# A two-block kernel with a written-out instruction order: the first third of the order is replaced

## The chip, the cores and the metric

The kernel runs on one core of a Trainium2 chip. The metric is the device time of one execution in microseconds (us). Five engines work side by side, each through its own instructions in a fixed order: TensorE (PE, with its weight loads shown as PEld), VectorE (DVE), ScalarE (ACT), GpSimd (POOL) and SyncE (SP), which here only issues DMAs. POOL issues DMAs too, and ACT issues eight at the start. An instruction waits, and everything behind it on its engine with it, until the results that it reads are there and the memory that it writes is free.

## The reference

Two blocks follow each other. The first is a linear recurrence over 768 time steps for 4 x 8 pairs of batch and head, with a 40 x 40 state in each:

```python
for t in range(S):
    kt, vt, rt = (k[:, :, t], v[:, :, t], r[:, :, t])
    wt, at, bt = (w[:, :, t], a[:, :, t], b[:, :, t])
    y[:, :, t] = np.einsum('bhd,bhde->bhe', rt, state)
    Sa = np.einsum('bhde,bhe->bhd', state, at)
    state_decay = state * wt[:, :, None, :] - np.einsum('bhd,bhe->bhde', Sa, bt)
    state = state_decay + np.einsum('bhd,bhe->bhde', vt, kt)
...
xn = x / rms * rms_g
g = xn @ w_gate
silu = g * (1.0 / (1.0 + np.exp(-g)))
val = xn @ w_val
return (silu * val @ w_out).astype(np.float32)
```

The second block (the lower five lines) takes the 3072 tokens of 320 values that the recurrence yields, normalises them, and puts them through a gated feed-forward layer with 1536 inner columns. The four weight arrays of this layer arrive as 64-bit floats.

## The kernel before

The 768 steps are cut into 24 chunks of 32. Inside a chunk the recurrence becomes matrix products and a triangular inverse. A chunk `c` goes through three stages, and every pair of chunks feeds the second block. In the text a piece is named by its stage and chunk, as "inverse 3".

- **front c** loads w, a, k, b, v of the chunk, turns them on PE, multiplies the decays up level by level (DVE, ACT), and forms products of keys and removals (`gramk`, 32 matmuls each on PE). At the end it writes a triangular matrix to DRAM (`sB<-LT`) and reads it back in another layout (`M<-sB`).
- **inverse c** inverts that triangle with short DVE operations. For the first four chunks (`early_inverse`) only two half-size triangles are inverted on DVE, which go out and back through DRAM (`sY<-M`, then four reads `M<-sY`); two matmul pieces `inv` on PE, with an ACT copy between them, join the halves. The first of the two reads what the four reads bring.
- **main c** applies the inverse to the incoming state, which waits for main c-1, updates the state, and computes the outputs of the chunk (`score`, `level`, `y0`), which are normalised and turned into `xg`.
- **feed g** runs for each pair of chunks through 12 blocks of inner columns: load a weight block (`wf<-sW`), products `h64` and `h`, Silu on ACT (`sg`), product with the value half on DVE (`hT`), product `out` on PE that accumulates in `po`.
- **narrow n** (24 pieces of work, all in the early part) turns the 64-bit weights into 32-bit ones: it loads raw words into a `wf` tile, takes three ACT and three DVE operations, and writes the result to the DRAM tile `sW`, from which `feed` reads.

None of this is issued in the order in which it is written. Each helper (`tt`, `copy`, `pe`, `dma` and so on) only records a piece in a `Plan`, with what it must wait for. At the end `plan.issue(ORDER, PAIRS)` goes through a long string of numbers. Each number is an offset from the first piece not yet issued, and says which piece is issued next, on whatever engine it belongs to. A dash issues a fill, a matmul that no result needs, which keeps PE at work:

```python
for word in order.split():
    if word == "-":
        self.order.append(None)
        self.warm()
        continue
    i = first + int(word)
...
plan.warm = lambda: nc.tensor.matmul(po_[:, 0, DM:DM + P], ident, ident, start=False, stop=False, skip_group_check=True)
```

The second string, `PAIRS`, says in which of three PSUM tile pairs each of 499 blocks of PE results (a "room") is placed. Between its issue and its use a piece has no other tie than its data, its memory and its neighbours on the engine. So `ORDER` sets for every engine and every DMA queue what stands behind what. All DVE operations carry line L444 in the profile, ACT copies L467, activations L464, scalings L470, DMA issues L483, matmuls L486, turns L489 and fills L1015, since the helpers stand there.

Of the kernel before, what the change touches and what calls it, by code (L numbers as in the profile page):

```python
# [33 lines left out]
78 84 86 83 5 88 73 58 85 74 60 77 59 87 89 53 61 76 90 4 75 80 43 6 7 62 8 334 - - - - - - 93 9 10 79 11 201 12 557  # L34
13 214 14 567 18 15 16 44 558 17 95 19 209 566 20 - 97 94 21 23 568 22 200 24 96 25 108 578 100 98 199 335 26 101 569
202 113 107 106 - - - - 102 54 577 112 213 111 125 210 122 110 124 586 103 120 46 559 2 57 104 52 560 109 598 105 - -
- - - - - - - - 114 588 561 45 118 119 27 562 123 116 392 589 563 132 204 121 117 134 212 129 131 136 135 47 564 570
597 203 - - - - - - - - - - 336 115 587 571 394 133 137 144 126 145 155 130 337 211 565 146 573 383 574 572 - 219 55
141 3 579 384 575 143 609 51 128 582 607 222 1005 127 580 281 608 583 48 220 381 339 234 81 142 390 239 221 251 - - -
- - - - - - - - - - 153 263 282 581 380 272 226 91 338 227 393 138 584 154 379 238 576 590 206 237 223 140 247 249 56  # L40
593 82 591 139 49 585 594 224 - 325 216 150 31 382 233 232 29 592 38 236 149 235 326 147 156 595 215 250 248 148 28
260 259 391 271 205 606 30 42 - - - - - - - - - 228 389 599 617 41 229 245 40 246 244 92 600 243 32 602 629 39 601 230
65 1006 1136 34 231 1414 627 37 66 152 603 35 50 - - - - - - - 240 151 610 71 604 628 611 64 613 63 241 252 262 36 614
258 69 242 356 261 0 69 255 256 71 254 617 611 398 269 32 625 98 67 253 66 267 266 206 268 604 252 207 278 400 614 636
217 399 647 401 263 216 405 279 156 595 413 877 406 648 402 265 157 868 417 0 0 257 719 0 258 269 0 242 454 706 265 0
0 0 263 0 - - - - - 242 247 0 262 0 263 462 0 243 462 0 0 272 0 460 0 0 266 0 264 0 275 239 0 461 248 0 245 441 238 0
86 247 441 0 229 95 93 441 0 229 93 95 0 242 0 467 450 0 268 227 - - - - - - - - - - - - - - - 236 467 0 437 467 0 0
38 0 254 435 0 209 233 88 252 199 249 232 - - 243 89 248 246 208 247 198 445 0 434 257 244 467 469 258 243 - 254 259
470 463 468 464 435 93 465 0 268 93 259 255 3 444 2 254 1 94 214 263 269 0 91 682 261 92 93 258 94 692 466 95 260 96
691 97 467 469 473 - - - - - 0 97 680 469 460 467 440 98 99 0 472 99 469 - 0 99 501 0 0 0 400 0 0 0 0 0 0 0 - - - - 20  # L50
0 0 0 0 19 150 147 0 17 150 0 144 0 375 356 0 13 352 358 16 359 356 - - - - - 25 357 17 26 360 80 148 394 149 18 29
150 81 396 151 192 393 70 27 395 31 152 71 30 153 361 154 386 0 35 31 - 189 27 388 154 386 389 190 36 387 37 45 192
390 34 391 155 32 33 156 396 157 158 0 396 398 3 158 - - - - - 37 399 2 397 1 159 45 160 40 0 157 34 37 551 158 159
560 160 396 210 549 38 429 39 161 552 212 42 430 162 561 397 163 43 164 550 213 44 559 165 45 - - - - - 0 561 45 46 0
164 565 165 166 167 168 46 169 566 740 567 580 739 47 572 568 729 573 429 - - - - - 0 729 582 429 47 583 48 431 0 381
- - 136 383 0 520 576 136 518 577 139 383 686 138 545 534 384 119 696 546 544 558 0 686 541 119 542 566 518 553 696
527 526 - - - - - - - 522 136 529 554 141 523 565 539 530 142 538 120 524 540 - - - - 145 525 537 534 154 152 148 536
149 556 555 121 - - 157 146 535 122 147 564 165 125 550 551 150 552 123 155 153 692 124 151 164 682 160 549 0 688 160
0 160 689 161 0 163 0 554 506 41 553 42 564 43 420 507 996 44 555 995 45 509 421 13 508 435 436 571 422 14 384 437 374
495 46 573 839 447 572 383 574 578 448 840 432 586 579 47 373 591 590 575 829 434 589 599 600 830 433 602 577 612 444  # L60
0 575 442 600 846 602 440 47 0 582 583 - 15 836 440 585 835 491 16 609 586 846 613 621 578 622 47 48 593 49 596 444
594 - 50 595 579 443 53 492 51 580 52 0 493 580 135 0 312 313 314 0 314 315 316 317 318 319 320 321 3 322 39 323 324
38 325 326 36 327 328 329 452 0 329 3 0 3 355 467 451 468 465 0 325 352 462 355 467 326 354 327 448 328 458 31 329 353
330 331 468 332 476 364 460 333 473 475 334 0 440 425 301 331 302 436 7 0 452 436 0 1 446 2 332 436 444 445 0 440 338
449 298 340 334 0 316 329 330 342 32 381 331 341 0 333 379 30 332 331 440 369 329 441 314 368 - - - - 0 442 294 441
518 295 0 297 295 335 0 0 331 27 37 46 1 28 336 337 29 36 30 338 31 34 341 2 342 294 3 0 647 439 440 441 637 442 443
444 646 335 31 445 446 645 336 447 448 449 634 28 0 607 310 35 311 606 0 258 307 7 610 308 29 618 259 416 309 27 417
28 418 310 419 619 821 281 420 421 620 633 812 621 625 311 811 638 - 475 0 311 625 821 281 636 635 312 0 648 644 1 647
0 418 0 - - - - - 4 642 643 654 619 309 5 310 653 825 418 665 657 419 824 420 26 666 421 422 815 9 27 29 44 814 30 45
28 42 423 0 616 423 5 32 424 9 6 33 470 425 617 10 0 419 303 420 421 465 0 614 300 301 418 615 419 0 401 12 0 282 598  # L70
32 597 590 21 401 402 33 403 464 3 22 591 0 219 0 399 587 0 599 0 7 586 217 8 0 598 8 9 0 457 598 396 599 32 9 35 397
398 0 0 - - - - - - - - - 582 23 388 22 389 390 32 597 600 3 604 598 33 599 447 14 603 583 391 4 15 612 17 0 579 13 11
387 388 14 20 389 15 390 417 0 38 22 20 37 23 2 418 35 390 417 391 47 419 392 393 420 394 21 395 396 588 0 27 23 2 396
0 21 585 600 601 599 586 27 25 0 31 418 27 25 393 394 595 419 395 28 52 396 29 596 422 397 597 607 398 604 0 397 571 0
394 571 391 577 0 363 1 5 387 2 577 394 364 392 0 362 377 386 0 384 394 507 569 377 392 506 568 387 571 497 401 647
570 496 402 0 394 416 395 377 705 396 713 359 400 397 378 712 0 400 713 401 701 402 654 714 403 404 0 702 655 1142 570
1143 656 571 701 572 654 573 574 8 575 404 576 577 0 577 639 404 578 579 405 580 2 406 581 582 407 583 584 357 585 408
781 586 360 587 717 588 358 3 0 588 358 589 639 718 975 590 3 717 591 0 980 588 637 719 715 981 589 720 0 587 967 406
715 713 728 986 416 724 588 976 401 589 714 729 0 984 589 740 590 591 974 402 721 403 662 401 592 722 752 717 726 738
# [968 lines left out]
```

## Time and profile before

| | |
|---|---|
| median of three runs | 1079.54 us (1079.13 to 1092.11) |
| the profiled execution | 1085.4 us, of which the span of the core's instructions is 1083.6 us |
| PE busy | 1021.8 us, 94% of the span |
| DVE busy | 851.0 us, 79% |
| ACT, POOL busy | 469.3 us and 308.9 us |
| granted PE clock, mean | 0.98 of full speed |
| DMA | 143.35 MB, mean 132 GB/s |

The profiled execution took 5.9 us more than the median. The busy share is an average over two quite different parts. In the first 240 us PE is idle or runs fills for a good part of the time, and the granted clock falls to half in five stretches. After that PE is hardly ever idle.

### The profile page before, as it was taken

What the parts mean: (1) busy time and instruction counts of PE and PEld (TensorE: products, weight loads), DVE (VectorE), ACT (ScalarE), POOL (GpSimd) and SP (SyncE); (2) the same over time, 40 slices, a digit from 0 to 9 for tenths busy, and PEclk for the clock granted to TensorE, in tenths of its full rate; (3) what the DMA queues carried; (4) which work ended last, traced back from release to release, by engine and by line L of the source; (5) the groups of instructions that cost most, each with busy time, mean ns of one, the idle gap of its engine ahead of it and who ended that gap; (6) DMA issues with size and microseconds to landing.
All of it is one profiled execution on the core that took longest, in us unless ns stands there. A gap on an engine that the chain in (4) does not pass through costs nothing.

```text
span 1083.6 us, 53520 instructions
## 1 busy us (share of the span) xinstructions
PE 1021.8 (94%) x23408; PEld 842.4 (78%) x23408; DVE 851.0 (79%) x2861; ACT 469.3 (43%) x1043; POOL 308.9 (29%) x554
## 2 busy tenths in 40 slices
PE   8877997899999999999999999999999999999998
PEld 7776776777877778787778778877878878887876
DVE  7877868885878988788798789979889889787321
ACT  5856755543543434433434334434335334432211
POOL 9714422120432141341332232332322331210000
PEclk9869998999999999999999999999989999999999
DMA  9965457775464483655555555555545555444242
GB/s 183 203 136 142 70 124 187 203 156 158 122 143 119 103 170 89 151 117 132 125 141 122 130 134 124 116 136 138 137 102 132 121 136 143 113 114 115 79 149 77
DMA packets 172458, 143.35 MB, mean 132 GB/s; under 512 B 125504, under 2 KB 143872, under 8 KB 172224
## 3 DMA queue, kind: packets, MB, share of 16 engines
q1 hardware_dynamic: 153856, 116.96, 42.2%
q0 software_dynamic: 16192, 22.64, 11.7%
q8 instruction: 184, 3.01, 1.2%
q10 hardware_dynamic: 2176, 0.33, 0.2%
q14 instruction: 50, 0.41, 0.1%
HBM read 123.86 MB, written 15.99 MB: 129 GB/s over the span
## 4 chain that ended last, share of the span: by engine, by line
PE 72%; DVE 12%; ACT 5%; DMA 4%; issue 4%; SPq 2%; POOL 0%; DVEq 0%; ACTq 0%; POOLq 0%
PE ps L486 49%; PE po L486 12%; PE ps L489 10%; DVE LT L444 2%; SPq L483 2%; DVE As L444 1%; DVE tmp L444 1%; DVE y L444 1%; DVE K L444 1%; DVE Yi L444 1%; ACT K L467 1%; DMA wf<-in_moe_w_val_dram 1%; PE po L1015 1%; DMA M<-sY 1%; ACT ex L464 1%
## 5 line engine op out<-in xcount | busy, mean ns | idle before, releaser
L486 PE MATMUL ps<-xg,wf 128*128 128x256 f32 (+1 forms) x1728 | 353.9, 391 | 5.2 <-DVE xg L444 2.1
L486 PEld LDWEIGHTS ps<-xg,wf 128*128 128x128 f32 (+1 forms) x1728 | 261.1, 188 | 60.3 <-issue 18.5
L486 PE MATMUL po<-wf,hT 128*128 128x320 f32 x576 | 180.0, 445 | 1.1 <-issue 0.6
L464 ACT ACTIVATE sg<-ps 128x256 f32<-128x256 f32 x144 | 53.7, 382 | 228.0 <-PE ps L486 215.5
L444 DVE TENSOR_TENSOR tmp<-Yi,M 128x60 f32<-128x60 f32 (+24 forms) x620 | 130.0, 210 | 20.1 <-DMA M<-sB 5.9
L483 POOL DMA_DIRECT2D VU<-in_v_dram x92 | 53.2, 584 | 310.3 <-PE ps L486 170.2
L444 DVE TENSOR_TENSOR Yi<-Yi,tmp 128x60 f32<-128x60 f32 (+24 forms) x620 | 129.8, 210 | 13.8
L486 PEld LDWEIGHTS po<-wf,hT 128*128 128x128 f32 x576 | 102.0, 189 | 36.6 <-issue 2.8
L444 DVE TENSOR_TENSOR hT<-ps,sg 128x256 f32<-128x256 f32 x144 | 59.6, 419 | 66.9 <-ACT sg L464 65.8
L444 DVE TENSOR_TENSOR K<-K,T 128x512 f32<-128x512 f32 (+1 forms) x192 | 93.1, 495 | 14.7 <-PE ps L486 5.7
L486 PEld LDWEIGHTS ps<-Ab,K 40*64 40x64 f32 x4608 | 78.6, 140 | 29.3 <-issue 10.2
L486 PE MATMUL ps<-Ab,K 40*64 40x56 f32 x4608 | 88.5, 227 | 8.9 <-issue 2.6
L467 ACT COPY K<-K 128x256 f32<-128x256 f32 (+1 forms) x168 | 70.8, 443 | 56.6 <-PE ps L486 34.8
L444 DVE TENSOR_TENSOR As<-ps,msi 128x256 f32<-128x256 f32 (+1 forms) x186 | 78.7, 474 | 15.7 <-PE ps L486 15.0
L467 ACT COPY KN<-ps 128x640 f32<-128x640 f32 x96 | 66.2, 690 | 54.5 <-PE ps L489 21.8
L483 POOL DMA_DIRECT2D kbn<-in_b_dram x92 | 53.8, 587 | 117.9 <-PE ps L486 109.6
L486 PEld LDWEIGHTS ps<-As,KN 128*40 128x40 f32 x3072 | 64.7, 122 | 15.9 <-issue 10.4
L486 PE MATMUL ps<-As,KN 128*40 128x32 f32 x3072 | 71.6, 203 | 3.5 <-issue 2.8
L483 POOL DMA_DIRECT2D kbn<-in_k_dram x92 | 53.5, 585 | 62.1 <-PE ps L486 62.1
L483 POOL DMA_DIRECT2D wn<-in_w_dram x92 | 51.5, 566 | 63.2 <-DVE KN L444 23.0
L444 DVE TENSOR_TENSOR y<-y,ps 128x256 f32<-128x256 f32 x119 | 49.9, 420 | 19.1 <-PE ps L486 16.7
L1015 PE MATMUL po<-ident 128*128 128x128 f32 x304 | 49.9, 318 | 7.0 <-issue 3.7
(133 smaller groups left out, 1571.3 us busy)
## 6 DMA issues: line engine op xcount, KB each, us to landing
wf<-sW SPq DMA_DIRECT2D x144, 480.0 KB, 4.0
M<-sB SPq DMA_DIRECT2D x80, 128.0 KB, 3.8
rn<-in_r_dram SPq DMA_DIRECT2D x24, 160.0 KB, 5.0
sW<-ex SPq DMA_DIRECT2D x16, 240.0 KB, 4.2
out_dram<-o SPq DMA_DIRECT2D x48, 80.0 KB, 4.6
kbn<-in_k_dram POOLq DMA_DIRECT2D x92, 40.0 KB, 3.8
kbn<-in_b_dram POOLq DMA_DIRECT2D x92, 40.0 KB, 3.8
wan<-in_w_dram POOLq DMA_DIRECT2D x46, 80.0 KB, 4.3
```

The source lines that it names most:

```text
L444: plan.add("DVE", kind, lambda at: fn(at(o), *m(at)), [o], aps(*args))
L464: plan.add("ACT", "act", lambda at: nc.scalar.activation(at(o), at(a), f, **kw), [o] + aps(acc), [a])
L467: plan.add("ACT", "copy", lambda at: nc.scalar.copy(at(o), at(a)), [o], [a])
L483: plan.add(by, "dma", lambda at: queue.dma_start(out=o, in_=i), [o], [i])
L486: return o, lhsT, rhs, lambda at: nc.tensor.matmul(at(o), lhsT, rhs, start=start, stop=stop, skip_group_check=True)
L489: return o, i, ident, lambda at: nc.tensor.transpose(at(o), i, ident)
L1015: plan.warm = lambda: nc.tensor.matmul(po_[:, 0, DM:DM + P], ident, ident, start=False, stop=False, skip_group_check=True)
```

## The change

Only the two strings differ. All pieces, their shapes, tiles, DMAs and data are the same.

`ORDER` has 6180 entries before and 6182 after. The last 4125 entries are the same piece for piece. The first 2055, which are 222 PE pieces, 797 DVE, 397 ACT, 231 POOL and 256 SP pieces and 152 fills, are issued in another order, with 154 fills. In the profile of before, that early part ends at 322 us of 1083.6 us. The core of the diff, the first lines of it, reads:

```diff
 ORDER = """
-78 84 86 83 5 88 73 58 85 74 60 77 59 87 89 53 61 76 90 4 75 80 43 6 7 62 8 334 - - - - - - 93 9 10 79 11 201 12 557
-13 214 14 567 18 15 16 44 558 17 95 19 209 566 20 - 97 94 21 23 568 22 200 24 96 25 108 578 100 98 199 335 26 101 569
...
```

`PAIRS` differs too. In the 354 blocks whose pieces all lie in the unchanged later part, the number of places in the order between the release of a pair and its next use is the same but for four blocks, so there the change is a renaming of the three pairs. In the early part the blocks follow the new order.

What the numbers mean on the engines can be read from the two orders. Counted by a piece's place on its own engine, most early pieces move little: 176 of 222 on PE, 288 of 397 on ACT and 485 of 797 on DVE move by at most three places. Five PE pieces move by more than ten. The moves that the prediction speaks of are these (place on its engine, before and after):

| piece | start before, us | place before | place after |
|---|---|---|---|
| inverse 3, first `inv` product, PE | 163.12 | 93 | 106 |
| inverse 3, second `inv` product, PE | 185.29 | 108 | 108 |
| narrow 15, first raw load, SP | 158.91 | 142 | 137 |
| inverse 3, last issued `M<-sY`, SP | 161.20 | 146 | 144 |
| main 3, product with `Xs`, PE | 196.63 | 112 | 109 |
| front 5, second `gramk`, PE | 191.77 | 109 | 110 |
| main 4, product with `Xs`, PE | 253.69 | 157 | 140 |
| main 4, turn of the state, PE | 274.48 | 176 | 198 |
| feed 2, first product, PE | 321.15 | 221 | 221 |

The fills move as well. Ahead of PE piece 51 there were 131 of them and there are 111; ahead of piece 67 there were 133 and there are 118; ahead of piece 111 there were 152 and there are 139. The last eleven of the new order stand just before the unchanged part: three before the first turn of front 8, four before its first `gramk`, and four before the first product of feed 2.

## Prediction

> **What bounds the kernel now.** I read the busy time by stretches first, since a new order for the first 322 us can only gain what that part loses. Columns: start and end, length, then busy us of PE, PEld, DVE, ACT and POOL with their instructions, the granted PE clock, DMA share, GB/s.
>
> ```profile
> 0.00:80.00 80.00, 64.03 (x1304) 59.24 (x1304) 66.06 (x202) 53.26 (x106) 49.70 (x109) 0.83 0.84 175
> 80.00:160.00 80.00, 69.64 (x2324) 59.66 (x2324) 62.38 (x186) 50.21 (x110) 28.65 (x52) 1.00 0.49 108
> 160.00:240.00 80.00, 68.60 (x1508) 56.27 (x1507) 66.03 (x223) 45.07 (x100) 22.27 (x38) 0.94 0.75 186
> 240.00:322.20 82.20, 80.13 (x1830) 64.19 (x1828) 56.34 (x194) 35.74 (x87) 24.62 (x42) 1.00 0.57 142
> 322.20:1083.60 761.40, 739.36 (x16447) 603.01 (x16446) 600.24 (x2059) 285.01 (x644) 183.68 (x314) 1.00 0.51 124
> ```
>
> PE is idle for 16.0, 10.4 and 11.4 us in the first three stretches, then for 2.1 us, and for 2.9% of the unchanged rest. That rest is bound by PE: whatever PE is early by at 322 us it keeps, if the rest runs as before. The same stretches for the fills alone (line L1015; PE and PEld only) show how much of the busy time is no work:
>
> ```profile
> 0.00:80.00 80.00, 33.43 (x200) 30.39 (x200) 0.83 0.84 175
> 80.00:160.00 80.00, 11.06 (x75) 9.18 (x74) 1.00 0.49 108
> 160.00:240.00 80.00, 5.45 (x30) 4.76 (x30) 0.94 0.75 186
> 240.00:322.20 82.20, 0.00 (x0) 0.00 (x0) 1.00 0.57 142
> ```
>
> So 322 us hold 39.8 us of idle PE and up to 49.9 us of fills, some 90 us without work, of which 49 lie in the first 80 us. There DVE is busy for 66 of 80 us: PE waits for chains through DVE and ACT, not the other way round.
>
> Then I read single waits, PE's timeline with the releaser in brackets:
>
> ```profile
> 40.78 1.08 PE L489 MATMUL ps<-ident,wan 128*104 128x128 f32 x8
> 45.78 1.11 PE L489 MATMUL ps<-ident,K 104*128 104x104 f32 x8 [3.92 <-DVE K L444]
> ...
> 166.96 0.79 PE L486 MATMUL ps<-M,LT 16*16 16x16 f32 x62 [3.62 <-DMA M<-sY]
> 167.76 1.92 PE L489 MATMUL ps<-ident,wan 128*104 128x128 f32 x8
> 169.47 1.06 PE L489 MATMUL ps<-ident,y 128*128 128x128 f32 x4
> ...
> 188.93 2.91 PE L1015 MATMUL po<-ident 128*128 128x128 f32 x16 [2.49 <-issue]
> ```
>
> The wait at 163 us is the clearest that an order can end: the first product of inverse 3 stands on PE for a DMA. The DMA is late because of its queue, as SP's own timeline shows:
>
> ```profile
> 154.59 2.25 SPq L483 DMA_DIRECT2D M<-sY  x3
> 158.91 0.47 SPq L483 DMA_DIRECT2D wf<-in_moe_w_val_dram  x1
> ...
> 161.20 0.43 SPq L483 DMA_DIRECT2D M<-sY  x1
> ```
>
> Three of the four reads go out by 156.8 us, the fourth at 161.2, behind a raw load that had waited, and the chain of waits holds the fourth with 5.71 us to its landing. The cost goes on after the wait: the same 8 turns take 1.92 us at 167.76 and 1.08 us at 40.78, and the granted clock says why:
>
> ```profile
> 165.80:172.60 6.80, 5.63 (x116) 5.30 (x117) 4.27 (x16) 3.15 (x9) 2.61 (x5) 0.50 0.90 227
> ```
>
> **The change part by part.** No instruction is removed or added but two fills, so every term is a wait that goes or comes. All are taken against the profiled execution: 1085.4 us, of which 1083.6 us are its span. The median of the runs is 5.9 us below it.
>
> **1. Up to 132 us: 0.** I add up what stands ahead of a PE piece on each engine, with its durations in this trace. Ahead of PE piece 66 (the turn of the normalised chunk 1, at 131.27 us), before and after: PE 73.6 and 73.6 us, DVE 124.8 and 125.1 us, ACT 100.0 and 100.0 us, SP 120 and 121 DMAs. Ahead of the turn that ends the longest wait above (45.78 us): DVE 42.0 and 42.2 us. The pieces that DVE had to get through before PE could go on are the same ones, a little permuted. The 15 fills that are taken out ahead of piece 67 are worth nothing where PE waits anyway. Bounds: DVE is idle for 7.7 us between 80 and 130 us (busy 42.31 of 50), so no more than some 8 us can be gained there. The loss is bounded by the clock: a half-clock stretch of 6.8 us holds up to 3.4 us of lost PE time, and two more of them would cost 7 us.
>
> **2. Inverse 3: -4.6 us.** Its first product moves 13 pieces back on PE, behind some 16 us of other work (109.6 us of PE work up to its end before, 125.7 after). In SP's order the held-up load now stands ahead of all four reads, and the PE piece that releases this load, a `feed` product, moves from place 84 to 82 ahead of other work and fills. So the reads go out at or before their old time, and land before PE comes to the product. The 3.62 us go. What is late next? The second product keeps its place (108) and ran at 185.3 us, 17 us after the first; now one `gramk` of 1.16 us stands between them, while the ACT copy between them takes 0.27 us. That should hold. Behind the wait PE also lost 0.84 us on the 8 turns and 1.2 us on the 12 further turns up to 171.9 us (1.06 and 1.59 us, against 0.60 and 0.88 us for the same ones at 279.71 and 274.48 us), together 2.0 us, to the half clock. DVE is busy 93% of the stretch from 160 to 165.8 us, so PE can't run far ahead of it: I take all of the wait and half of the 2.0 us. Ends: -5.6 us, and 0 if DVE sets the pace.
>
> **3. Around 186 to 192 us: -1 us.** Between 186.0 us and the second `gramk` of front 5 at 191.77 us PE runs nine fills and stands 2.49 us for nothing that the profile names. The `gramk` had its last input at 189.75 us (ACT K) and then stood behind fills at half clock. Afterwards five fills, the 0.78 us product of main 3, and one fill stand there. The product fills 0.8 us that were empty, and three fills fewer stand ahead of the `gramk`. Ends: 0 and -2.0 us.
>
> **4. 200 to 310 us: 0.** The main 4 pieces that move by 17 and 16 places go ahead of `feed` work that PE had ready, so PE has the same sum to do with 0.5 us idle. The idle 2.6 and 1.8 us of 200 to 220 and 220 to 240 us have the same waits and places (DMA `M<-sB` at 214 us, SP place 194 in both). Ends: -2 and +2 us.
>
> **5. The join at 322 us: +1.4 us.** Eleven fills stand in the last ten pieces where there were none. At full clock ten fills took 2.5 us (13.53 us, 20 matmuls in 2.50 us), so eleven are 2.7 us; a gap of 1.29 us stood before the first product of feed 2, in whose place four of them come. Hidden if PE waits there as long anyway, so ends 0 and +2.7 us.
>
> Sum: 0 - 4.6 - 1 + 0 + 1.4 = -4.2 us. That is 1081.2 us for an execution like the profiled one, and 1079.5 - 4.2 = **1075.3 us** against the median. The outer ends add up to -17.6 and +11.7 us, but they will not all fall on one side.
>
> **A rule against the change.** The trace has five half-clock stretches (29.3, 46.3, 63.4, 165.8 and 189.7 us; 3.4, 6.8, 17, 6.8 and 3.4 us long), and each starts within 4 us after PE stood still for 1.7 us or more, in one case 3.92 us. [...]
>
> **The rivals.**
>
> A. *Slower: the clock falls between 80 and 130 us.* That stretch now runs at 1.00, with 31 fills between PE pieces 26 (80.15 us) and 51 (116.40 us). In the new order 16 stand there. If a pause of 1.7 us is left open between PE pieces 40 and 60, two stretches of 6.8 us at half clock cost up to 7 us. With the rest of the sum, -4.2 + 7 = +2.8 us: 1082.3 us. For: before there were seven fills ahead of the first `gramk` of front 3 (108.26 us) and none remains. Against: DVE and ACT work ahead of these pieces is 1 us less, so the pause may be shorter too.
>
> B. *Larger gain.* Of 51 pairs of a DMA and its reader in which the reader started less than 1.5 us after the landing, 35 stand further apart in the new order and 14 closer. If that takes out the small waits too, the idle 21.8 us of 80 to 240 us could fall towards the 2.9% of the later part, 4.6 us. That is -17 us: 1062 us. Against it: DVE's busy 128 of these 160 us, and the pauses put down to "issue" (9.9 us of PE in the first 240 us), which an order can't be seen to end.
>
> C. *No change: given back at the join.* The late order expects blocks and buffers at the time they had. If PE comes 4 us early and then stands for front 8 and feed 2, as eleven fills there suggest, the result is 1079.5 us, give or take 2.
>
> D. *It doesn't do what it says.* New issue times shift DMAs that share one set of engines (share 0.84 in the first 80 us), so the landing times that the order was made for don't come again. A tight read such as `narrow 23`'s raw load (23 places apart before, 17 now, 0.15 us to spare) then stalls ACT by about 1 us each. Five such stalls cost 5 us and eat the gain: 1080.3 us.
>
> **How the numbers follow.** Forecast 0.45, A 0.15, B 0.12, C 0.18, D 0.10. The range leaves out the far ends of A and B: 1063 to 1087 us; the forecast's own is 1069 to 1079 us. A change of 2% (21.6 us) is about what a measurement of this kernel can tell from no change. To be faster by that, a quarter of the 90 us without work must go, though 49 of them lie where nothing that counts moves: 0.04. Slower by it needs three times A's price: 0.03. Within 2%: 0.93.
>
> **What would show it.** Right: no wait of 3.6 us on `M<-sY` around 160 us, PE at the `Xs` product of main 3 before 194 us, feed 2's first product at 316 to 320 us, the rest 761 us long as before, turns of 1.08 us around 165 us. Wrong: a granted clock of 0.5 between 80 and 130 us (A), PE idle below 30 us before 322 us (B), feed 2's first product early but the rest longer (C), new waits of ACT or DVE on raw loads (D). The largest single doubt is term 1.

## The result, and the profile after

| | before | after |
|---|---|---|
| median, measured side by side | 1085.41 us (1078.41 to 1094.88) | 1096.83 us (1088.70 to 1107.54) |
| ratio, with its 95% interval | | 1.0105 (1.0077 to 1.0132) |
| the profiled execution | 1085.4 us | 1094.2 us |
| its span, mean granted clock | 1083.6 us, 0.980 | 1092.4 us, 0.971 |
| end of the first product of feed 2 (the join) | 322.21 us | 328.69 us |
| from there to the end | 761.4 us | 763.7 us |

The new order is 1% slower, 11 us, where 4 us faster were forecast. The medians of before move between 1080 and 1087 us from one series to the next (the three runs shown at first gave 1079.5), so every ratio below is against runs of before in the same series. Ratios leave out the executions that ran over 1.5% above the fastest of the same kernel; medians don't.

The stretches of after, columns as before (the stretch, its length, then busy us of PE, PEld, DVE, ACT and POOL, the granted clock, DMA share, GB/s):

```profile
0.00:80.00 80.00, 60.55 (x1231) 55.83 (x1231) 68.23 (x201) 51.43 (x102) 49.11 (x107) 0.83 0.87 177
80.00:160.00 80.00, 69.43 (x2199) 59.57 (x2201) 58.65 (x180) 49.93 (x110) 26.16 (x48) 0.87 0.42 88
160.00:240.00 80.00, 72.02 (x1688) 58.24 (x1684) 65.04 (x220) 48.83 (x104) 25.20 (x43) 1.00 0.80 204
240.00:328.70 88.70, 85.43 (x1861) 69.42 (x1861) 61.29 (x203) 34.38 (x85) 24.69 (x42) 1.00 0.53 135
328.70:1092.40 763.70, 742.70 (x16448) 604.85 (x16446) 601.56 (x2060) 285.66 (x644) 183.68 (x314) 0.99 0.51 123
```

The clock between 80 and 160 us fell from 1.00 to 0.87, and rose from 0.94 to 1.00 between 160 and 240. In the first 80 us PE has 3.5 us less to show. PE's timeline at the waits that the prediction spoke of, and at two new ones:

```profile
14.11 1.16 PE L486 MATMUL ps<-A,K 40*64 40x56 f32 x64 [2.95 <-DVE A L444]
...
66.23 1.62 PE L489 MATMUL ps<-ident,K 104*128 104x104 f32 x8 [4.47 <-DVE K L444]
...
187.49 0.69 PE L486 MATMUL ps<-M,LT 16*16 16x16 f32 x64
188.11 1.16 PE L486 MATMUL ps<-A,K 40*64 40x56 f32 x64
189.19 0.73 PE L486 MATMUL ps<-M 16*32 16x16 f32 x64
...
191.77 0.42 PE L486 MATMUL ps<-Xs,M 32*32 32x40 f32 x25 [0.54 <-ACT M L467]
193.52 0.56 PE L486 MATMUL ps<-Xs,M 32*32 32x40 f32 x39 [1.33 <-issue]
```

SP's timeline, at the four reads:

```profile
165.17 0.79 SPq L483 DMA_DIRECT2D M<-sY  x2
...
166.48 1.50 SPq L483 DMA_DIRECT2D M<-sY  x2
```

And the fills of after (line L1015), by the first four of the stretches above (PE, PEld, clock, DMA share, GB/s):

```profile
0.00:80.00 80.00, 30.71 (x184) 27.62 (x184) 0.83 0.87 177
80.00:160.00 80.00, 10.02 (x52) 7.96 (x52) 0.87 0.42 88
160.00:240.00 80.00, 8.01 (x50) 6.64 (x50) 1.00 0.80 204
240.00:328.70 88.70, 2.97 (x22) 2.69 (x22) 1.00 0.53 135
```

The fills moved from the first 160 us, 3.8 us less, to later, 5.5 us more. Inverse 3's first product (187.49) no longer waits, and main 3's `Xs` product came at 191.77 instead of 196.63 us. That part went as forecast. The first two lines are waits for DVE's chain that were shorter or not there: in before the same `gramk` of front 0 came at 12.44 us without a wait, and in the place of the 4.47 us the last `gramk` of front 2 waited 1.74 us:

```profile
12.44 1.15 PE L486 MATMUL ps<-A,K 40*64 40x56 f32 x64
...
62.58 1.33 PE L486 MATMUL ps<-Ab,K 40*64 40x56 f32 x64 [1.74 <-DVE K L444]
```

To add up where 6.5 us went ahead of the join, I cut both traces at PE pieces up to which both orders have issued the same set, and take the length of each stretch (us, from the ends of the pieces in the two timelines). In this and the later tables by stretches PE pieces are counted from 1; the places in the edits below, as in the tables ahead of the result, count from 0.

| PE pieces | before | after | what differs in after |
|---|---|---|---|
| 1 to 24 | 71.2 | 76.7 | waits for DVE 17.4 instead of 13.4, fills 1.7 more |
| 25 to 46 | 39.2 | 37.6 | fills 5.5 less, but 20.5 us at half clock instead of 9.2 |
| 47 to 93 | 52.8 | 56.2 | pauses put down to issue 4.4 instead of 1.8 |
| 94 to 108 | 22.2 | 18.8 | no DMA wait (3.6) |
| 109 to 140 | 45.0 | 41.6 | pauses put down to issue 1.3 instead of 3.5 |
| 141 to 167 | 35.6 | 36.6 | fills 0.9 |
| 168 to 219 | 52.5 | 56.4 | pauses put down to issue 2.7 instead of 0.3, fills 0.7 |
| 220 to 222 | 3.8 | 4.8 | fills 1.8, wait for ACT 1.0 less |

By kind, up to the join: PE's work 242.5 us instead of 237.4 (47.8 us at half clock instead of 37.5), waits for DVE 21.5 instead of 15.2, for DMAs 1.6 instead of 5.1, for ACT 7.1 instead of 8.7, issue 11.1 and 10.8, fills 44.9 and 45.1 (where no other matmul runs beside them, so less than the busy time above). Pieces 94 to 140 gain 6.8 us in this trace; the other stretches lose 13.2. All of this is one execution of each kernel.

### The profile page after: what moved, and what is told of

Its sections match the earlier page's. It is cut to its first block, busy times and chain, and to the rows that moved or that the text cites. A ratio compares the mean times of both kernels' runs of the same rounds, so it can differ in the third digit from the quotient of the medians.

```text
span 1092.4 us, 53529 instructions
## 1 busy us (share of the span) xinstructions
PE 1030.1 (94%) x23412; PEld 847.9 (78%) x23412; DVE 854.8 (78%) x2861; ACT 470.2 (43%) x1043; POOL 308.8 (28%) x554
## 4 chain that ended last, share of the span: by engine, by line
PE 72%; DVE 13%; DMA 5%; issue 4%; ACT 3%; SPq 2%; POOL 1%; DVEq 0%; ACTq 0%; POOLq 0%
PE ps L486 50%; PE po L486 12%; PE ps L489 9%; DVE LT L444 2%; DMA sW<-ex 2%; SPq L483 2%; DVE tmp L444 1%; DVE Yi L444 1%; DVE y L444 1%; DVE K L444 1%; PE po L1015 1%; DVE As L444 1%; DMA sY<-Yi 1%; DVE hT L444 1%; DVE wf L444 1%
## 5 line engine op out<-in xcount | busy, mean ns | idle before, releaser
L486 PE MATMUL ps<-xg,wf 128*128 128x256 f32 (+1 forms) x1728 | 356.8, 394 | 3.4 <-DVE xg L444 2.1
L486 PEld LDWEIGHTS ps<-xg,wf 128*128 128x128 f32 (+1 forms) x1728 | 263.0, 190 | 60.1 <-issue 16.0
L486 PE MATMUL po<-wf,hT 128*128 128x320 f32 x576 | 179.0, 444 | 2.1 <-issue 1.3
L444 DVE TENSOR_TENSOR tmp<-Yi,M 128x60 f32<-128x60 f32 (+24 forms) x620 | 130.5, 211 | 17.1 <-DMA M<-sB 2.9
L444 DVE TENSOR_TENSOR Yi<-Yi,tmp 128x60 f32<-128x60 f32 (+24 forms) x620 | 130.1, 210 | 14.2 <-DVE tmp L444 0.2
L486 PEld LDWEIGHTS po<-wf,hT 128*128 128x128 f32 x576 | 102.5, 190 | 37.6 <-issue 3.2
L444 DVE TENSOR_TENSOR hT<-ps,sg 128x256 f32<-128x256 f32 x144 | 59.5, 420 | 63.9 <-ACT sg L464 62.8
L444 DVE TENSOR_TENSOR K<-K,T 128x512 f32<-128x512 f32 (+1 forms) x192 | 95.3, 504 | 14.1 <-PE ps L486 6.8
L486 PEld LDWEIGHTS ps<-Ab,K 40*64 40x64 f32 x4608 | 79.1, 140 | 26.0 <-issue 7.7
L486 PE MATMUL ps<-Ab,K 40*64 40x56 f32 x4608 | 89.0, 227 | 6.9 <-DVE LT L444 1.9
L467 ACT COPY K<-K 128x256 f32<-128x256 f32 (+1 forms) x168 | 71.3, 443 | 54.6 <-PE ps L486 35.1
L444 DVE TENSOR_TENSOR As<-ps,msi 128x256 f32<-128x256 f32 (+1 forms) x186 | 78.4, 477 | 18.4 <-PE ps L486 15.7
L486 PEld LDWEIGHTS ps<-As,KN 128*40 128x40 f32 x3072 | 66.9, 124 | 22.3 <-issue 11.2
L486 PE MATMUL ps<-As,KN 128*40 128x32 f32 x3072 | 75.0, 205 | 8.3 <-issue 3.5
L483 POOL DMA_DIRECT2D wn<-in_w_dram x92 | 51.4, 564 | 63.9 <-DVE Yi L444 21.5
L1015 PE MATMUL po<-ident 128*128 128x128 f32 x308 | 51.7, 316 | 3.3 <-DVE po L517 3.3
```

What stands on the lines that cost most here:

```text
L444: plan.add("DVE", kind, lambda at: fn(at(o), *m(at)), [o], aps(*args))
L467: plan.add("ACT", "copy", lambda at: nc.scalar.copy(at(o), at(a)), [o], [a])
L483: plan.add(by, "dma", lambda at: queue.dma_start(out=o, in_=i), [o], [i])
L486: return o, lhsT, rhs, lambda at: nc.tensor.matmul(at(o), lhsT, rhs, start=start, stop=stop, skip_group_check=True)
```

## The experiments

All kernels compute the same as the two orders. In kernels with another `ORDER` string the helpers' lines move by up to five (L484 for L486).

**Pieces or fills.** First the two ingredients of the change were crossed: the new order of the pieces with the old numbers of fills at each place of PE, and the reverse.

```diff
 e1: pieces of the new order
-fills ahead of PE pieces 0, 2, 3, 4, 5, 6 ...: 7, 7, 4, 4, 1, 6 ... (154)
+fills ahead of PE pieces 0, 1, 2, 3, 4, 6 ...: 6, 1, 4, 10, 10, 1 ... (152)
 e2: pieces of the old order, with the fills of the new (154)
```

> The new order of pieces, with the 152 fills of before, each standing ahead of the same PE place as before. Theory Clock (the loss is PE time at half clock, since the new order has fewer fills between PE pieces 26 and 66): half-clock time up to the join falls from 47.8 us to about 37 us, and the ratio to before falls from 1.0105 to about 1.005 or less. Theory Start (the loss is made by the order of the first 80 us, where DVE stands 3 us behind POOL memsets and inverse 0 comes 5 us later): the ratio stays at 1.008 to 1.013.

> The order of pieces of before, with the 154 fills of the new order, each standing ahead of the same PE place as there. Theory Clock: half-clock time up to the join rises by some 10 us and the ratio to before is about 1.005. Theory Start: 1.000, within 0.003.

Measured: e1 1114.29 us, ratio 1.0199 (1.0137 to 1.0261); e2 1099.13 us, 1.0131 (1.0090 to 1.0172). Both lie outside what either theory allowed. Either ingredient alone costs as much as both or more, so neither is the harmful one by itself. In both kernels the pieces and the fills seem to fit each other.

**First 640 entries from one order, the others from the other.**

```diff
 e3: entries 0 to 639 old, then the new order (159 fills)
 e4: entries 0 to 639 new, then the old order (147 fills)
```

> The first 640 entries of the old order (up to PE piece 27, some 81 us), then everything else in the new order. Theory Start: the loss is gone, ratio 1.000 to 1.003, and the first product of feed 2 comes at about 322 to 324 us. Theory Clock, or any theory by which the part from 81 to 322 us makes the loss: ratio 1.007 to 1.012.

> The first 640 entries of the new order (up to PE piece 26, some 87 us in its profile), then everything else in the old order. Theory Start: the loss is there, ratio 1.007 to 1.012. Theory Clock or a later loss: ratio 1.000 to 1.005.

Measured: e3 1107.08 us, 1.0190 (1.0137 to 1.0243); e4 1095.91 us, 1.0065 (1.0031 to 1.0099). Here the rest after the join, whose instructions are the same in all kernels, was not as long: 774.6 us in e3 and 762.9 in e4, against 761.4. That spoils the comparison, and opens a second question.

**More fills, or none.** Fills were added in the pauses that the traces showed, or all taken out.

```diff
 e5: old order
+80 fills, as 6 ahead of PE piece 7, 15 ahead of 15, 8 ahead of 23, 14 ahead of 93 ...
 e6: new order
+103 fills, as 11 ahead of PE piece 2, 14 ahead of 15, 17 ahead of 21 ...
 e7: old order, e8: new order
-all fills (152 and 154)
```

> The order of before with 80 more fills, put in front of the PE pieces ahead of which its profile shows PE idle for 0.7 us or more (one fill per 0.24 us of the pause). Over all runs so far each us at half clock goes with 0.41 us of time. Theory Clock: half-clock time per run falls from 53 us to 35 us or less, ratio to before 0.990 to 0.995. Theory Waits (fills delay the piece behind them, and the clock follows the waits and doesn't make them): ratio 1.000 or more.

> The new order with 103 more fills, put in the pauses of its own profile in the same way. Theory Clock: half-clock time per run falls from 66 us to 45 us or less, ratio to before 0.998 to 1.004 (it was 1.0105). Theory Waits: ratio 1.010 or more.

> The order of before without any fill. Theory Clock: half-clock time per run over 130 us, and some 0.41 us for each us above 53, so a ratio of 1.03 or more. Theory Waits: PE waits in any case, ratio 0.998 to 1.005.

> The new order without any fill, to be compared with the old order without any. If the new order's own waits make part of the loss whatever the clock does, it is 3 to 6 us slower than the old order without fills. If all of the loss comes from where the fills stand, the two are within 3 us of each other.

Measured: e5 1.0263 (1.0204 to 1.0323), e6 1.0437 (1.0377 to 1.0496), e7 1.0331 (1.0256 to 1.0406), e8 1.0591 (1.0524 to 1.0658). In e6 the time at half clock ahead of the join fell from 47.8 to 17.1 us and idle PE from 41.3 to 30.4, but the fills took 18.4 us more: the join stayed at 328.6. So fills put into waits are not free: 18.4 us of them took away 10.9 us of idle time. Without any fill the new order is still slower than the old one, by more than the 3 to 6 us expected (1.0591 against 1.0331), so it doesn't lose only by where its fills stand. The rest grew to 780.2, 797.5, 800.7 and 793.6 us (e5 and e6 have five of their fills in it, and e7's profiled execution was 16 us above its median).

The idle time that grows there is put down to issue by the profile. The views of PE's waits in the rest, first of before, then of e5 (total us, times, longest):

```profile
PE ps L486 <- issue: 5.8, 11, 1.3
PE po L486 <- issue: 0.6, 1, 0.6
```

```profile
PE ps L485 <- issue: 14.6, 20, 1.2
```

**Where these pauses stand.** I numbered PE's instructions in the order of issue: two for each matmul (it and its weight load) and one for each wait of PE's sequencer. In the twenty traces there are 397 pauses of over 0.3 us put down to issue, together 418 us; 385 of them, 407 us, stand at four neighbouring places of 256, nearly all at 192 or 193. PE of before has 23,408 matmuls, as many weight loads and 316 others, 47,132 or 184.1 times 256, and the page lists for its instruction queue (packets, MB, share):

```profile
q8 instruction: 184, 3.01, 1.2%
```

All of these packets have 16,384 bytes, 64 for each of 256 instructions. In before a pause ends this long after such a packet has:

| pause ends, us | PE instruction, and its place in 256 | packet's end | between |
|---|---|---|---|
| 76.28 | 2496, 192 | 75.03 | 1.25 |
| 90.01 | 3265, 193 | 88.58 | 1.43 |
| 98.68 | 3777, 193 | 97.20 | 1.48 |
| 132.88 | 5825, 193 | 131.48 | 1.39 |
| 188.93 | 8384, 192 | 187.48 | 1.45 |

Over all 18 pauses at block ends in before it is 1.43 us, give or take 0.11. By these times PE stands for its next block of 256 instructions, and runs on 1.4 us after the block's packet has ended. It is mostly quick blocks that make it wait. Two products of 64 small matmuls with their weight loads (0.7 to 1.2 us each) fill a block. Counted over the twenty traces, 197 of the 443 blocks that PE got through in less than 3.5 us end in a pause of over 0.3 us, and 24 of the 1872 that took it over 5 us. A quick block alone doesn't decide: in before one of 2.09 us (from 468.7 us) ended without a pause. At most cuts nothing of the kind shows: only 18 of some 184 in before have a pause of over 0.3 us. These 18 hold 15.2 us, and those of e8 38.0.

A fill is two matmuls and two weight loads. So each fill ahead moves all later cuts by four instructions, and 64 fills bring the old cuts back. These four kernels tested that: seven fills more at the very start, 64 more in waits before 140 us, three fewer at the start, and, for the forecast's join, the eleven late fills moved to the start.

```diff
 e10
-78 84 86 ... 62 8 334 - - - - - - 93 9 10
+78 84 86 ... 62 8 334 - - - - - - - - - - - - - 93 9 10
 e14
-78 84 86 ... 62 8 334 - - - - - - 93 9 10
+78 84 86 ... 62 8 334 - - - 93 9 10
 e13: old order
+64 fills: 6, 15, 6, 8, 6, 3, 2, 3, 14, 1 ahead of PE pieces 7, 15, 21, 23, 38, 44, 67, 83, 93, 123
 e11: new order
-3, 4 and 4 fills ahead of PE pieces 214, 219, 221
+11 fills ahead of PE piece 0
```

> The old order with seven more fills at its very start, where PE waits 3.3 us for its first input anyway: 159 fills instead of 152, no other difference. Theory (the length of the unchanged rest hangs on how many PE instructions stand ahead of it, through pauses of PE that nothing in the profile causes): the rest after the join is 770 to 778 us, as in the other kernel with 159 fills (774.6), pauses put down to issue in the rest are 8 to 11 us instead of 6.6, and the time is 8 to 14 us above before. Rival (the long rest of that other kernel came from its other placing of blocks in the three PSUM pairs): the rest is 761 to 764 us, the join within 2 us of 322, and the time that of before within 3 us.

> The old order with 64 more fills, spread over places where PE waits before 140 us; 216 fills instead of 152, that is 256 more PE instructions (a fill is two matmuls and two weight loads) ahead of the join. In all traces so far the pauses of PE that are put down to issue stand at every 256th PE instruction (place 192 or 193 of each 256), and end 1.4 us after a 16,384-byte packet of PE's instruction queue. Theory (these pauses depend on where the 256-instruction blocks are cut, so 256 more bring the old cuts back): the rest after the join is 760 to 764 us and holds 5 to 8 us of issue pauses, as with 152 fills, though there are more fills than with 159 (775 us) and nearly as many as with 232 (780 us, 16.7 us). Rival (each PE instruction ahead costs the rest something, or the fills' mere number does): rest above 772 us and issue pauses above 12 us. The join comes some us later than before, since not all of the fills fit into waits: 324 to 332 us.

> The old order with three of its six first fills left out: 149 instead of 152, all else the same. Theory (block cuts): a replay of the old trace's PE times with a block released 4.2 us after PE's sequencer enters the block before it gives 5.4 us of issue pauses in the rest at 152 fills, 3.6 at 149 and 14.7 at 159 (measured 6.6 and 11.5 for 152 and 159). So the rest is 1 to 3 us shorter than 761.4, the early part the same within 2 us, and the time 1 to 3 us below before: the candidate for a version below both kernels. Rival (the early part needs these fills): the join later by 3 us or more, and the time above before.

> The new order, its eleven fills of the last ten early pieces moved to the very start; 154 fills as in the new order. Theory (the term for the join was right: these fills take PE time there): the join comes 1.4 to 2.7 us earlier than in the new order (326 to 327.3 us against 328.7), and the time falls by as much, to 1092 to 1094 us where the new order has 1096. Rival (PE waits there for its inputs anyway): join and time unchanged within 1 us. By the theory on PE instructions ahead, the rest stays at 763 to 764 us, since their number is the same.

| kernel | fills | rest, us | of it issue pauses | at half clock | ratio to before |
|---|---|---|---|---|---|
| e14 | 149 | 758.3 | 5.3 | 0.3 | 1.0019 (0.9984 to 1.0053) |
| before | 152 | 761.4 | 6.6 | 6.8 | |
| e10 | 159 | 775.3 | 11.5 | 21.1 | 1.0190 (1.0147 to 1.0234) |
| e13 | 216 | 764.8 | 5.7 | 16.3 | 1.0067 (1.0037 to 1.0098) |
| e5 | 232 | 780.2 | 16.7 | 16.1 | 1.0263 (1.0204 to 1.0323) |
| e11 | 154 | 764.7 | 5.8 | 17.2 | 1.0168 (1.0137 to 1.0200) |

PE's waits for issue in the rest of e13, with 64 fills more than before:

```profile
PE ps L485 <- issue: 3.8, 8, 0.7
...
PE po L485 <- issue: 1.4, 1, 1.4
...
PE ps L488 <- issue: 0.4, 1, 0.4
```

Seven fills nearly doubled the pauses, 64 did nothing to them. The place of the cuts decides, not the number. Three other kernels bear this out: e1, e15 and e18, whose early parts differ, have six, seven and eight PE instructions fewer ahead of the join than before has, and each shows one pause of 3.1 to 4.2 us at 272 to 275 us behind the join. No kernel with 12, 4, 2 or no instructions fewer shows one there. The pauses are not all of it: of the 13.9 us by which e10's rest is longer, 4.9 are these pauses, and some 4.7 its 14.3 us more at half clock, at the price worked out next. The other 4 are not accounted for. The rest of e13 is 0.8 us beyond its expected range, for another reason: its clock. In nine kernels whose cuts differ from those of before by less than thirteen instructions, and whose rest has 5.3 to 6.6 us of issue pauses, the rest goes up with its time at half clock: 758.3 us at 0.3 (e14), 760.5 at 0 (e12), 758.9 at 2.8 (e17), 761.3 at 5.6 (e16), 761.4 at 6.8, 763.6 at 14.2 (e9), 763.7 at 15.4 (after), 764.8 at 16.3 (e13), 764.7 at 17.2 (e11). A line through them rises by 0.33 us for each us at half clock. (e1, e15 and e18, with 7.8 to 9.4 us of pauses, lie 4 to 5 us above it; e2, with 5.0, lies on it.) e14's profiled execution is the shortest of all (span 1078.7 us, join 320.4), but its median is that of before: what it may gain is less than these runs can tell.

e11 and e10 also showed an error of mine. PE's first fills wait for a DVE memset of `po` until 3.31 us, so fills at the start don't lie in a wait: the first turn came at 8.73 us in e10 and 9.69 in e11, against 6.92 and 6.77. e11's join at 336.9 us says therefore nothing on the late fills.

**One part alone: inverse 3's first product.**

```diff
 PE pieces of the old order
 feed0.21 out
-inverse3.40 inv      (and, on ACT, its copy)
 front5.20 turn
 ...
 feed0.32 out
+inverse3.40 inv      (and, on ACT, its copy)
 front5.29 gramk
```

> The old order with one part of the change alone: the first product of inverse 3 and its copy stand 13 PE pieces later, as in the new order; all fills and all else as before. Theory (the step of the sum was right, its gain is lost elsewhere in the new order): the wait of 3.62 us on the read M<-sY goes, the half-clock stretch behind it goes, the join comes 3.6 to 5.6 us earlier (317 to 319 us in the profile against 322.2), the rest stays 761 us, and the time is 4 to 5 us below the kernel before. Rival 1 (the wait only hid another one: DVE and ACT set the pace of this stretch): the wait goes, another takes its place within 10 us, the join is at 321 to 323 us and the time is the same within 2 us. Rival 2 (every new place brings its own half-clock stretches): the mean half-clock time rises by 10 us or more, and the time by 4 us or more.

Measured: 1088.67 us, 1.0014 (0.9980 to 1.0047); join 323.20, rest 763.6. The wait on `M<-sY` went, but nothing was gained. PE's timeline of e9:

```profile
170.07 0.66 PE L487 MATMUL ps<-ident,y 128*128 128x128 f32 x4 [2.16 <-DVE y L442]
...
185.01 0.68 PE L484 MATMUL ps<-M,LT 16*16 16x16 f32 x64
185.62 1.16 PE L484 MATMUL ps<-A,K 40*64 40x56 f32 x64
...
187.54 0.72 PE L484 MATMUL ps<-M 16*32 16x16 f32 x64
188.19 0.49 PE L1013 MATMUL po<-ident 128*128 128x128 f32 x2
192.72 1.65 PE L1013 MATMUL po<-ident 128*128 128x128 f32 x7 [4.04 <-issue]
```

In the place of 3.62 us come 2.16 us for DVE, and the pause at the block's end, at 188.9 us in before, grows from 2.49 to 4.04 us: 2.16 + 1.55 = 3.71. The product now stands with two others of 64 matmuls, and PE gets through the block before in 1.78 us, where it took 4.42. The packet of that block started at 190.47 us and ended at 191.43. This kernel is also a measure of chance: up to piece 93 it is the old order, and came there 3.8 us later than before did, e14 0.5 us later, e17 0.2 us earlier. Single profiles can't settle less than some 4 us.

**POOL's memsets.** After's first long wait, 2.95 us at 11 us, was for DVE operations that took 2 to 3 us instead of 0.2 to 0.7. First DVE, then POOL in after:

```profile
10.32 3.21 DVE L444 TENSOR_SCALAR near<-vut 128x32 f32<-128x32 int32 x3
10.58 2.94 DVE L444 TENSOR_TENSOR T<-T 128x256 f32<-128x256 f32 x1
10.92 2.61 DVE L444 TENSOR_TENSOR A<-A,T 128x256 f32<-128x256 f32 x1
11.27 2.25 DVE L444 TENSOR_TENSOR K<-K,T 128x512 f32<-128x512 f32 x1
```

```profile
10.84 0.25 POOL L479 MEMSET msi<- 128x160 f32 x1
11.00 0.97 POOL L479 MEMSET ST<- 128x1024 f32 x1
11.90 0.65 POOL L479 MEMSET wn<- 128x640 f32 x1
12.47 0.97 POOL L479 MEMSET ST<- 128x1024 f32 x1
```

All six DVE operations end between 13.48 and 13.53 us, the last memset at 13.44. The first starts at 10.32 us, half a us before the first memset, while POOL issues a DMA (10.20 to 10.85 us). The first of the six has a single input (`near<-vut`), and the ones with two inputs stand behind it. That DVE and POOL end together, within 0.1 us, doesn't yet show that one holds the other. e12 moves three memsets:

```diff
 POOL, new order
 msi
-ST, wn, ST
 load of w, load of b, load of b, ... load of k
+ST
 rn, M, load of b
+wn
 ... load of k
+ST
```

> The new order, with three POOL memsets (two ST, one wn) of 11 to 13.4 us moved later on POOL, as before had them, so that no four memsets stand back to back; 154 fills, all else as in the new order. Theory (POOL's memsets hold up DVE, and PE loses its first three microseconds to that): the six DVE operations that took 2.3 to 3.2 us take 0.2 to 0.7 us, PE's pause of 2.95 us at 11.2 us falls to 1.8 us or less, the half-clock stretch at 15.5 us goes, and the join comes 2 to 4 us earlier, with the time as much below the new order. Rival 1 (DVE was late for another reason): the six operations stay above 2 us. Rival 2 (the start is waited for again further on): the operations are short, but the join is within 1 us of 328.7 and the time within 2 us of the new order.

DVE in e12:

```profile
10.54 0.35 DVE L442 TENSOR_SCALAR near<-vut 128x32 f32<-128x32 int32 x3
10.80 0.42 DVE L442 TENSOR_TENSOR T<-T 128x256 f32<-128x256 f32 x1
11.14 0.44 DVE L442 TENSOR_TENSOR A<-A,T 128x256 f32<-128x256 f32 x1
11.49 0.69 DVE L442 TENSOR_TENSOR K<-K,T 128x512 f32<-128x512 f32 x1
```

The memsets are shown to be what held DVE there, and PE's pause fell to 1.79 us. But the edit made the same hold again further on, since `wn` now stands in a row with three other memsets (`wn`, `LT`, `kbn`, `VU`, 17.38 to 19.21 us). DVE in e12 beside them:

```profile
16.91 2.76 DVE L442 TENSOR_SCALAR wf<-wf 128x480 int32<-128x480 int32 x1
```

In after that DVE operation took 1.04 us. The time of e12 is 1094.39 us, 1.0082 (1.0046 to 1.0117), not clearly below the new order; 17.1 us at half clock began at 14.3 us, a DMA was waited for at 20.4 us (3.12), and the join was at 335.4. Of rival 2 the short operations and the missing gain came; a join within 1 us of 328.7 did not. So e12 moves the hold more than it removes it, and what the hold costs the kernel stays open.

**The halves again, with the fills brought to 152.**

```diff
 e15: entries 0 to 639 old, then new
-7 of the 11 late fills
 e16: entries 0 to 639 new, then old
+5 fills ahead of PE piece 21
```

> The first 640 entries (some 80 us, 28 PE pieces) in the old order, the rest of the early part in the new one, brought to 152 fills by leaving out seven of the eleven at the join; the later blocks keep the new order's succession in the three PSUM pairs, so the cuts in the unchanged rest are those of before. The earlier mix of this kind had 159 fills and a rest of 774.6 us, which hid the answer. Theory (what the new order loses lies in its first 80 us): join 322 to 325 us, rest 761 to 764, time within 3 us of before. Rival (it lies after 80 us): join 327 to 333 us, and the time 5 to 10 us above before.

> The reverse mix: the first 640 entries in the new order, then the old one, with five fills added in PE's wait for the turn of chunk 1's K (43 to 47 us), 152 in all, and the old succession of the later blocks in the pairs. Theory (the loss lies in the first 80 us): join 326 to 330 us, time 5 to 10 us above before. Rival (it lies after 80 us): join 322 to 325 us, time within 3 us of before. If both mixes are above before by half as much, the loss is spread; if both are above by as much as the new order, every departure from the old places costs the same, whatever it is.

Measured: e15 1098.34 us, 1.0144 (1.0106 to 1.0182), join 336.7, rest 765.6; e16 1092.09 us, 1.0070 (1.0044 to 1.0097), join 333.3, rest 761.3. (e16's five fills in fact stand in the wait for chunk 2's K.) Both halves lose, and more together than the whole: neither theory holds. Of the outcomes named there the last is the nearest, that every departure from the old places costs, though not the same: e15 costs more than the new order and e16 less. With as many fills as before, e15 still has seven instructions fewer ahead of the join, waits of PE's sequencer; its rest has 8.7 us of issue pauses.

**The winning stretch alone, and the losing tail taken away.**

```diff
 e17: old order; PE pieces 93 to 140, and the other engines' between, in the new one (152 fills)
 e18: new order; from PE piece 167 to the join the old one
+4 and 5 fills ahead of PE pieces 15 and 21 (152)
```

> The old order with the new one only from PE piece 93 to 140 (163 to 230 us; all engines' entries of that stretch), 152 fills. In the traces this is the stretch in which the new order wins: it was 7.3 us behind at piece 93 and 0.6 us behind at piece 140. Theory (the gain belongs to this stretch and is lost in others): from piece 93 to 140 PE takes 60 to 63 us against 67.1 before, the lead of 4 to 7 us stays to the join (316 to 319 us), the rest is 759 to 763, and the time is 4 to 6 us below before, 1080 to 1082 us: below both kernels. Rival (the gain in this stretch was only the catching up of a PE that came late, when its inputs had long been there): PE comes to piece 93 early, waits for the same inputs as before, and the join is at 321 to 324 us with the time of before within 3 us.

> The new order up to PE piece 167 (267 us), then the old order to the join, so without the eleven fills there; nine fills more in PE's waits for the turns of K of chunks 1 and 2, 152 in all. Theory (between pieces 167 and 222 the new order loses 5 us, by 2.4 us more of pauses at the ends of PE's instruction blocks, since eight products of 64 small matmuls stand close together there, and by 2.5 us of fills): this stretch takes 56 to 57 us against 61.3 in the new order and 56.3 before, the join is at 322 to 326 us and the time 3 to 6 us below the new order, 1090 to 1093 us. Rival (the stretch is as long, since what it waits for came late): 60 us or more, and the time of the new order within 2 us.

| PE pieces, us | before | after | e15 | e16 | e17 | e18 |
|---|---|---|---|---|---|---|
| 1 to 24 | 71.2 | 76.7 | 73.8 | 81.8 | 72.8 | 77.1 |
| 47 to 93 | 52.8 | 56.2 | 62.2 | 55.4 | 52.7 | 58.4 |
| 94 to 140 | 67.2 | 60.5 | 63.9 | 65.8 | 66.6 | 63.4 |
| 168 to 219 | 52.5 | 56.4 | 58.6 | 53.2 | 52.6 | 54.6 |

e17: 1084.77 us, 1.0029 (1.0002 to 1.0057). The stretch that took 60.5 us in after takes 66.6 with the same order when PE comes to it on time (162.97 us at piece 93, not 170.5). The rival holds, with a join at 320.6 us where it had 321 to 324: after's gain there was the catching up of a PE that was late. e18: 1098.41 us, 1.0166 (1.0123 to 1.0209). Its last stretch, pieces 168 to 222, took 57.4 us instead of 61.3, near what was expected, but pieces 47 to 93 took 2.2 us more than in after, the join stayed at 328.7, and the rest was 768.2 us with 9.4 us of issue pauses (eight instructions fewer stand ahead of it, so that its cuts come eight later than those of before).

Two losses come again wherever the new order stands. Pieces 1 to 24 take 76.7 to 81.8 us in it (after, e12, e16, e18) and 71.2 to 73.8 in the old one (before, e9, e14, e15, e17). Pieces 168 to 219 take 56.4 to 58.6 us (after, e12, e15) and 52.3 to 53.2 (before, e9, e14, e16, e17), with 2.5 to 2.7 us of issue pauses against 0 to 0.6.

## Why the prediction was wrong, by its own steps

**The time.** 1075.3 us was forecast, 1063 to 1087, and 1096.8 measured. Within 2% of before, which had most of the chance, is true; the sign is not.

**Term 1 (first 132 us: 0, from -8 to +7) failed.** At the turn of the normalised chunk 1, up to which it was counted, after is 6.4 us late (137.71 us against 131.27), and at piece 93 7.3 us: the upper end, where nothing was forecast. The sums of what stands ahead of a piece on each engine were equal, but they don't tell what a chain waits for: six of DVE's operations took 2 to 3 us at the start, and front 2's turn of K stood ahead of its last `gramk` and waited 4.47 us. That the start alone costs is shown by e16 (1.0070); which of its waits does is not: moving the clearest one (e12) brought nothing that can be told.

**Rival A came, at chance 0.15.** The clock between 80 and 160 us fell to 0.87. Half clock began at 94.0 us after a pause of 0.99 us (at 90.7), at 107.6 in one of 1.44 us (at 106.4), at 138.4 after one of 1.13 us (at 135.5). Between 80 and 130 us 17.3 us were at half clock, where there was half a us: two new stretches of 6.8 and 3.4 us, and 7.1 us of one that began at 76.9. A change that takes fills out had to carry this in its sum, not as a rival. It is not all of the loss: the rival's own time was 1082.3 us. Nor was its condition met, a pause of 1.7 us; and in before pauses of 1.20 us (at 88.8) and 1.66 us (at 97.0) were followed by no half clock. So the length of a pause alone doesn't decide, and what does stays open. Over 228 of the executions that the ratios use, each against its own kernel's mean, a us more at half clock (twice the missing share of the clock, times the time) goes with 0.25 us more time (correlation 0.63). In these after has 64 us at half clock in the mean, before 46 to 52 in five series. At 0.25 to 0.33 us each, these 12 to 18 us more would be 3 to 6 of the 11 us; that they cause them is argued, not shown.

**Term 2 (-4.6 us) was right in place and nearly in size, and wrong as a gain.** Pieces 94 to 108 took 3.4 us less, and the wait went. The reads `M<-sY` did not go out at their old time (154.6 to 161.2 us) but from 165.2 to 168.0 us, and still landed before PE came at 187.5. By itself the move is worth nothing (e9: 1.0014), nor is the stretch (e17: 1.0029). The step that failed is "whatever PE is early by it keeps": a PE that isn't late waits there for DVE, and for its next block of instructions.

**Term 3 (-1 us)** held: pieces 109 to 120 took 20.4 us instead of 22.2.

**Term 4 (0, from -2 to +2) was mis-sized:** pieces 121 to 219 took 3.3 us more. PE had its inputs, as forecast; it lost 2.4 us more at block ends from piece 168 on. Its four pauses there stand in pieces 205 to 217, and 205 to 219 are all small products of 32 or 64 matmuls and turns (main 5's last products for the most part), where in the old order `feed` products stand among them. That issue pauses are something "which an order can't be seen to end", as rival B has it, was the error behind it: the order sets which instructions fill a block of 256.

**Term 5 (+1.4 us, 0 to 2.7)** is +1.0 us for pieces 220 to 222.

**"The rest as before" held, by luck: the new cuts fall two instructions from the old ones.** 763.7 instead of 761.4 us, with 5.5 us of issue pauses instead of 6.6 and 15.4 us at half clock instead of 6.8. With seven fills more, which the sum would have priced at nothing, the rest is 14 us longer (e10).

What stays open: how the 11 us divide, how the loss of the first 24 pieces divides among its waits, and why half an order loses more than a whole one. No kernel here is below before; e14, e17 and e9 can't be told from it or are slightly above.

## What to carry to other kernels

A wait removed by an order is worth what is left when the engine comes on time: move the one piece alone, and see whether the next wait takes its place. Number the instructions of a busy engine, and look where its unexplained pauses stand; if they come at one place of 256 (here 385 of 397 over 0.3 us stand at four neighbouring ones), look at what the cuts do before judging two orders by their times: a few fills shift them (seven took the issue pauses of the rest from 6.6 to 11.5 us in e10). That spreading the small instructions ends such pauses is not tried here. Compare orders only with the same count of instructions ahead of what they share.

## What the runs showed of the hardware that was not expected

- Nearly all of PE's pauses over 0.3 us without a shown cause (385 of 397) stand at the ends of blocks of 256 instructions, up to 4.16 us long (e18); in before they end 1.43 us after the 16,384-byte packet of the next block. A replay of before's PE times with one rule (a block is ready 4.2 us after PE is 32 instructions ahead of the cut before it; both numbers fitted) gives the issue pauses of the rest in the twenty kernels, 5 to 24.5 us, with correlation 0.95. That rests on the kernels whose cuts lie far from those of before: for e14 the replay gave 3.6 us, and 5.3 were measured.
- Half clock began in after behind pauses of 0.99 and 1.13 us and in one of 1.44 us, while pauses of 1.20 and 1.66 us in before were followed by none. In the PE-bound rest, with the same instructions, each us of it went with 0.33 us (nine kernels).
- Four POOL memsets in a row (2.6 us) held six DVE operations until the last one ended; with three of them elsewhere these took 0.17 to 0.69 us. Another row of four (17.38 to 19.21 us in e12) held a TENSOR_SCALAR for 2.76 us. A single memset beside a two-input operation held nothing: in e12 `K<-K,T` took 0.45 us at 15.87, within a memset from 15.30 to 16.27.
